# A six-layer feature-cross network rewritten: four groups in flight, batched tails, a row-major last job

## The chip, the cores and the metric

The kernel runs on one core of one Trainium2 chip. The metric is the device time of a run in microseconds (us); a time quoted for a kernel is the median of its runs. The profiled span of a run is some 2 us shorter than its device time, so spans are compared only with spans.

## The reference

```python
B, D, L = 16384, 416, 6        # x0: (B, D), ws: (L, D, D), bs: (L, D), all bf16
x = x0
for l in range(L):
    proj = x @ ws[l] + bs[l]
    x = x0 * proj + x
return x
```

416 is 3 × 128 + 32. The 32 left-over features (the *tail*) shape both kernels: an array of 128 by 128 has to be divided into strips to be used well by them.

## The kernel before

The rows are cut into eight groups of 2048. Inside, the features lie on the partitions, so x is held transposed: three tiles of 128 × 2048, and the tail folded as 128 × 512 (four chunks of 512 rows, 32 features each). One *job* is one layer of one group. TensorE (PE) fills banks of 512 columns in PSUM (the memory that matmuls write to), ScalarE (ACT) *evicts* them, that is, copies them to a buffer in SBUF (the on-chip working memory) with the bias added, and VectorE (DVE) multiplies by x0 and adds x. A *ring* is a set of such buffers used in turn. The core of a job on PE (cut: lines and indentation left out):

```python
for i in range(NMT):                       # three output tiles of 128 features
    rp_first = (i % 2 == 1)
    if rp_first:                           # the 32-row matmuls first, then 12 full ones
        emit_k32(g, l, i, xin3, nb_of, False, first=True)
        emit_full(g, l, i, xin, nb_of, waits_tj, k32_first=True)
    else:
        emit_full(g, l, i, xin, nb_of, waits_tj)
        emit_k32(g, l, i, xin3, nb_of, False)
emit_tail_cp(g, l, xin, jb["tail"])        # the tail: 12 matmuls of 32 columns
emit_tail_bd(g, l, xin3, jb["tail"])       # and one with a block-diagonal weight
```

Four 32-row matmuls run at once in four strips of the array, so a job is 43 *passes* of 512 columns: 3 × (12 + 1) for the tiles, 3 + 1 for the tail. Two groups are in flight at a time. ACT evicts 512 columns at a time into a ring of three wide buffers and, for tails, a ring of two.

```python
NTW = 3      # wide eviction buffers, 128 x 2048
NTS = 2      # tail eviction buffers, 128 x 512
...
for n, bk in enumerate(banks):
    act.wait_ge(sem_pe, n + 1)
    if n == e["first_bank"] and e["ring_wait"]:
        ...
        if e["ring"] == "s" and e["rk"] >= NTS:
            act.wait_ge(sem_dve, small_list[e["rk"] - NTS] + 1)
    ...
    act.activation(dst, src, ACT_F.Identity, bias=bias_ap, scale=1.0).then_inc(sem_act, 1)
```

All x0 come by transposing DMAs from DRAM. The outputs of groups 0 to 5 go through a DRAM scratch and a transposing DMA back; the last two groups are transposed on PE at the end and stored by rows.

## Time and profile before

The time before is 512.78 us (three runs, 512.35 to 512.87). How to read the profile: PE, DVE, ACT and POOL are engines, PEld is the loading of weights for PE, the granted clock is the share of PE's full clock that the chip allowed it at the time ("cold" below means matmuls at a low granted clock), and the "chain" is the chain of work that ended last, followed back from the end. The first fence has lines of the page of the kernel before: its span, busy time by engine, and the chain's shares.

```profile
span 511.6 us, 7778 instructions
...
PE 485.9 (95%) x3069; PEld 198.8 (39%) x3118; DVE 376.9 (74%) x430; ACT 381.9 (75%) x646; POOL 9.5 (2%) x36
...
PE 89%; DVE 3%; issue 2%; DMA 2%; ACT 2%; SPq 1%; DVEq 0%; ACTq 0%
```

PE is busy 95% of the time and carries 89% of the chain. The next fence is the timeline of PE in the kernel before, in mid-run. Its columns: start in us, length in us, engine, line, operation, output and inputs, shape, how many, and in brackets how long the engine stood idle before.

```profile
211.28 0.39 PE L526 MATMUL ps<-x_3_1,w_3 32*128 32x512 bf16 x4
211.60 1.04 PE L504 MATMUL ps<-x_1_0,w_0 128*128 128x512 bf16 x4
...
216.89 0.39 PE L528 MATMUL ps<-x_3_1,w_3 32*128 32x512 bf16 x4
217.21 0.40 PE L539 MATMUL ps<-x_1_0,w_0 128*32 128x512 bf16 x4
...
218.20 1.03 PE L504 MATMUL ps<-x_0_0,w_0 128*128 128x512 bf16 x4 [0.16 <-issue]
```

A job repeats every 9.83 us without a stall. Its 43 passes at 0.216 us are 9.29 us; the rest is five changes of shape (128 rows to 32 rows, to 32 columns, and back) at about 0.105 us each. The Trainium skill ("TensorEngine Tiling (Array Packing)", Key Properties) says that changing the tiling mode drains TensorE; it gives no figure, and this trace agrees and prices it.

The third fence is the view by windows of the kernel before: window, its length, then busy time and number of instructions of PE, PEld, DVE, ACT and POOL, then the granted PE clock, the DMA share and GB/s.

```profile
0.00:27.53 27.53, 19.61 (x91) 7.90 (x93) 3.61 (x4) 8.36 (x14) 2.40 (x16) 1.00 0.86 149
122.34:495.16 372.82, 366.21 (x2285) 147.60 (x2323) 291.79 (x319) 294.72 (x497) 0.00 (x0) 1.00 0.43 107
495.16:511.60 16.44, 7.08 (x128) 6.05 (x127) 10.34 (x34) 7.11 (x16) 0.00 (x0) 0.86 0.65 208
```

In the middle DVE is busy 78% (291.79 of 372.82) and ACT 79%. The second job starts at 27.53, and 16.4 us pass after the last regular matmul (that is, the last matmul of a job, not a transpose of the output).

### The profile page before, as it was taken

To read this page: it belongs to the slowest core of one execution; us is meant where nothing else is said; L and a number is where in the kernel's file an instruction comes from. 1 tells how busy PE (TensorE), PEld (TensorE's weight loads), DVE (VectorE), ACT (ScalarE), POOL (GpSimd) and SP (SyncE) were. 2 spreads that over 40 slices of the span, in tenths; PEclk is the share of its full clock that TensorE was granted. 3 is DMA by queue.
4 is the path that set the end of the run, shared out by engine and by line. 5 is a ranking of instruction groups with operands and counts; after the bars stand their busy time and mean duration, and the time that the engine had idled before them with its cause. 6 is when DMAs were issued, how large, how long until landed. Compare 5 with 4: busy or idle time off the path is not lost.

```text
span 511.6 us, 7778 instructions
## 1 busy us (share of the span) xinstructions
PE 485.9 (95%) x3069; PEld 198.8 (39%) x3118; DVE 376.9 (74%) x430; ACT 381.9 (75%) x646; POOL 9.5 (2%) x36
## 2 busy tenths in 40 slices
PE   5899999999999999999999999999999999999992
PEld 2333343343334334343433433343343343434352
DVE  0167787787788778778787877877887787787795
ACT  1467787787878778787877878787787777878782
POOL 1020200000000000000000000000000000000000
PEclk9999999999999999999999999999999999999998
DMA  9769700000667799000569579000277660000008
GB/s 168 153 150 206 142 2 0 1 1 1 176 168 233 159 209 190 1 0 2 163 156 247 136 200 215 15 2 1 57 218 217 184 168 0 1 1 0 1 2 266
DMA packets 134147, 53.91 MB, mean 105 GB/s; under 512 B 111584, under 2 KB 131808, under 8 KB 134112
## 3 DMA queue, kind: packets, MB, share of 16 engines
q1 hardware_dynamic: 128252, 51.29, 41.9%
q10 hardware_dynamic: 5860, 2.14, 1.8%
q8 instruction: 24, 0.39, 0.3%
q14 instruction: 11, 0.09, 0.0%
HBM read 2.56 MB, written 23.86 MB: 52 GB/s over the span
## 4 chain that ended last, share of the span: by engine, by line
PE 89%; DVE 3%; issue 2%; DMA 2%; ACT 2%; SPq 1%; DVEq 0%; ACTq 0%
PE ps L504 74%; PE ps L539 7%; PE ps L528 6%; PE ps L526 2%; DMA x0T_2<-in_x_dram 2%; ACT tmpw L420 2%; SPq L243 1%; DVE tmpw L743 1%; DVE x_0_1 L704 0%; PE ps L485 0%; DVE x_0_2 L704 0%; DVE x_1_1 L773 0%; DVE x_0_0 L704 0%; PE ps L656 0%; DVE tmpw L738 0%
## 5 line engine op out<-in xcount | busy, mean ns | idle before, releaser
L420 ACT ACTIVATE tmpw<-ps,bias_f 128x512 bf16<-128x512 f32 x576 | 343.7, 698 | 107.4 <-PE ps L528 107.4
L738 DVE TENSOR_TENSOR tmpw<-tmpw,x0T_2 128x2048 bf16<-128x2048 bf16 x47 | 57.6, 1225 | 51.9 <-ACT tmpw L420 51.9
L738 DVE TENSOR_TENSOR tmpw<-tmpw,x0T_1 128x2048 bf16<-128x2048 bf16 x47 | 57.6, 1226 | 48.2 <-ACT tmpw L420 48.2
L738 DVE TENSOR_TENSOR tmpw<-tmpw,x0T_0 128x2048 bf16<-128x2048 bf16 x47 | 57.3, 1219 | 28.6 <-ACT tmpw L420 28.1
L504 PE MATMUL ps<-x_1_0,w_0 128*128 128x512 bf16 x287 | 74.0, 380 | 3.3 <-issue 3.2
L504 PE MATMUL ps<-x_1_1,w_1 128*128 128x512 bf16 x288 | 73.9, 379 | 0.0
L504 PE MATMUL ps<-x_1_2,w_2 128*128 128x512 bf16 x288 | 73.9, 379 | 0.0
L504 PE MATMUL ps<-x_0_0,w_0 128*128 128x512 bf16 x192 | 49.4, 380 | 2.6 <-issue 2.6
L504 PE MATMUL ps<-x_0_1,w_1 128*128 128x512 bf16 x192 | 49.3, 379 | 0.0
L504 PE MATMUL ps<-x_0_2,w_2 128*128 128x512 bf16 x192 | 49.3, 379 | 0.0
L504 PEld LDWEIGHTS ps<-x_1_1,w_1 128*128 128x128 bf16 x288 | 28.2, 98 | 34.0
L504 PEld LDWEIGHTS ps<-x_1_2,w_2 128*128 128x128 bf16 x288 | 28.2, 98 | 34.0
L504 PEld LDWEIGHTS ps<-x_1_0,w_0 128*128 128x128 bf16 x288 | 25.9, 98 | 36.1 <-issue 10.2
L420 ACT ACTIVATE tmps<-ps,bias_f 128x512 bf16<-128x512 f32 x48 | 33.9, 705 | 0.0
L704 DVE TENSOR_TENSOR x_0_0<-tmpw,x_1_0 128x2048 bf16<-128x2048 bf16 (+1 forms) x27 | 29.7, 1099 | 0.0
L704 DVE TENSOR_TENSOR x_0_1<-tmpw,x_1_1 128x2048 bf16<-128x2048 bf16 (+1 forms) x27 | 29.7, 1099 | 0.0
L704 DVE TENSOR_TENSOR x_0_2<-tmpw,x_1_2 128x2048 bf16<-128x2048 bf16 (+1 forms) x27 | 29.7, 1099 | 0.0
L504 PE MATMUL ps<-x0T_0,w_0 128*128 128x512 bf16 x95 | 27.0, 402 | 2.8 <-DMA w_2<-in_ws_dram 1.4
L504 PE MATMUL ps<-x0T_1,w_1 128*128 128x512 bf16 x95 | 26.2, 399 | 3.2 <-DMA x0T_1<-in_x_dram 3.2
L504 PEld LDWEIGHTS ps<-x_0_2,w_2 128*128 128x128 bf16 x192 | 18.8, 98 | 22.7
L504 PEld LDWEIGHTS ps<-x_0_1,w_1 128*128 128x128 bf16 x192 | 18.8, 98 | 22.7
L504 PEld LDWEIGHTS ps<-x_0_0,w_0 128*128 128x128 bf16 x192 | 17.5, 98 | 23.8 <-issue 6.8
(204 smaller groups left out, 393.9 us busy)
## 6 DMA issues: line engine op xcount, KB each, us to landing
out_dram<-ost SPq DMA_DIRECT2D x25, 416.0 KB, 3.4
x6T_scratch<-x_0_0 SPq DMA_DIRECT2D x6, 512.0 KB
x6T_scratch<-x_0_1 SPq DMA_DIRECT2D x6, 512.0 KB
x6T_scratch<-x_0_2 SPq DMA_DIRECT2D x6, 512.0 KB
w_1<-in_ws_dram SPq DMA_DIRECT2D x6, 104.0 KB
w_2<-in_ws_dram SPq DMA_DIRECT2D x6, 104.0 KB
w_0<-in_ws_dram SPq DMA_DIRECT2D x5, 104.0 KB
out_dram<-x_1_0 SPq DMA_DIRECT2D x1, 416.0 KB, 2.7
```

Source lines behind the costliest of these rows:

```text
L243: sp.dma_start_transpose(x0T[s][t][:, :], x0[0:GC, t * P:(t + 1) * P]).then_inc(sem_g0[t], 16)
L420: act.activation(dst, src, ACT_F.Identity, bias=bias_ap, scale=1.0).then_inc(sem_act, 1)
L504: ins = pe.matmul(bank_ap(nb_of[(i, j)]), wm[l][t][:, ecols], xin[t][:, j * CH:(j + 1) * CH], start=(t == 0 and not k32_first), stop=last,)
L526: pe.matmul(bank_ap(nb_of[(i, j)]), lhsT, rhs, start=True, stop=False, tile_position=tp)
L528: pe.matmul(bank_ap(nb_of[(i, j)]), lhsT, rhs, start=False, stop=True, tile_position=tp).then_inc(sem_pe, 1)
L539: ins = pe.matmul(bank_ap(n, j * TAIL, (j + 1) * TAIL), wm[l][t][:, ecols], xin[t][:, j * CH:(j + 1) * CH], start=(t == 0 and not bd_first ...
L704: dve.tensor_tensor(o_ap, t_ap, i_ap, ALU.add).then_inc(sem_dve, 1)
L738: dve.tensor_tensor(tw[:, :], tw[:, :], x0T[s][i][:, :], ALU.mult).then_inc(sem_dm, 1)
L743: dve.tensor_tensor(tw[:, cols], tw[:, cols], x0T[s][i][:, cols], ALU.mult).then_inc(sem_dm, 1)
```

## The change

The intent is to change shape less often, to start and end sooner, and to need no DRAM scratch. The whole kernel is rewritten (a small scheduler derives the waits), so the diff is cut to its core.

1. *Staggered groups.* Jobs run on a diagonal order over up to four groups, so that the tails of four jobs can run in one phase, and 24 full matmuls run between 32-row phases of eight.

```diff
-for r in range(NR):
-    for l in range(L):
-        for q in range(R):
-            units.append(("job", r * R + q, l))
+order = [(0, 0), (0, 1), (1, 0), (0, 2), (1, 1), (2, 0), (0, 3), (1, 2), (2, 1), (3, 0), ...]
+cuts = [1, 2, 3, 4, 4, 4, 4, 4, 4, 4, 4, 4, 3, 2]          # tails per batch
+def tails(batch):
+    bs_ = take(len(batch))                                  # one PSUM bank for each tail
+    for (g, l), b in zip(batch, bs_):
+        ...   # 12 matmuls of 32 columns, 4 with the block-diagonal weight
+        evacuate_tail(g, l, b)                              # ACT, then two DVE instructions
```

2. *Eviction.* ACT mostly takes 1024 columns at a time. Wide buffers go from 3 to 4, tail buffers from 2 to 3. DVE's add of one eviction is held back until after the multiply of the next.

```diff
-    NTW = 3
-    NTS = 2
+    NX0, NXS, NX3, NTW, NTS = 5, 6, 8, 4, 3
+        add("act", ... activation(ts[r][:, :], bank(b), ...), writes=[("ts", r)])       # r: one of NTS
+        add("dve", ... tensor_tensor(ts[r], ts[r], x0 tail, mult), release=True)
+        add("dve", ... tensor_tensor(x3s[so], ts[r], src, add), hold=True)
```

3. *Start.* Group 0 comes by plain loads and is transposed on PE. Layer 1's weights are queued behind group 1, whose tail is copied inside SBUF and waits for a transposing DMA.

```diff
-for t in range(NMT):
-    load_x0_tile_g0(t)                     # transposing DMAs
+for j in range(NJ):
+    add("sp", ... dma_start(x0n[:, j, :, :], perm(g0, j)))   # plain; PE transposes
+load_group(1)                              # 4 transposing DMAs, 4 copies that wait for the last
+load_w(1, "sp")
+load_w(2, "sp")
```

4. *Outputs* of groups 0 to 6: DMA transposes from SBUF to SBUF, then one store of 1.7 MB, all on the sync engine's (SP) queue.

5. *The last job* (group 7, layer 5) is computed with rows on the partitions, so that its result needs no transpose. The bias then varies along the free axis, and comes as one more matmul of a row of ones with a bias row (`brow`). Four passes; each multiplies by the rows of x0 and adds the rows of x.

```diff
+# done_with(g, l), at the end of a group's last layer
+if l == L - 1:
+    output(g)                                              # transposes, then the store
+...
+# after all regular jobs
+for j in range(NJ):
+    add("sp", ... dma_start(x0n7[:, j, :, :], perm(rows7, j)))             # x0 rows of group 7
+    add("sp", ... dma_start(brow[j * T32:j * T32 + 1, :], bs[l:l + 1, :])) # bias row
+for kk in range(KK):
+    if kk % 2 == 0:
+        for j in range(NJ): nat_full(kk, j, bks[j], True)
+        nat_rows(kk, bks, False)                           # needs brow
+        if kk == 0: to_rows(0)                             # PE transposes of x, copied by ACT and DVE
+        for j in range(NJ): nat_out(kk, j, bks[j])         # ACT copy, DVE multiply and add
+    ...
```

## The prediction

> **What bounds the kernel now.** TensorE. The page has PE busy 95% of 511.6 us; the chain of waits is 89% PE. In the timeline at 200 to 230 us a job (one group, one layer) repeats every 9.83 us without a stall: 43 passes of 512 columns at 0.216 us and five changes of tiling shape at about 0.105 us (12 full passes to the 32-row phase: 2.69 us, 2.59 of it passes). The Trainium skill ("TensorEngine Tiling (Array Packing)", Key Properties) says that a mode change drains TensorE; this trace agrees and prices it. ACT and DVE have slack (windows: 79% and 78% busy in the middle). The start costs 17.7 us (second job at 27.53, less 9.83), the end 16.4 us (last regular matmul 495.16, span 511.6).
>
> **Middle.** Counted from the instruction order, shape changes fall from 256 to 169: -9.1 us. The 32x32 tail-copy phases (0.43 us for each of six groups) go: -2.6 us. One of 48 jobs moves into the row-major finish; the 47 others take about 455 us of PE, 9.69 us a job. ACT evicts mostly 1024 columns at a time; DVE keeps about 8 us a job. Neither should bind; I expect PE gap-free.
>
> **Start.** Group 0 comes by plain loads (1.7 MB; plain DMA reached 325 GB/s in the windows at the end) instead of DMA transposes (2.3 to 3.1 us per 512 KB). Data by 9 us, PE transposes and copies to 11, first job to 22.5 with a cold clock. The weights of layer 1 sit on SP behind four DMA transposes and copies that wait for the last: they land near 25, so the second job starts near 25 instead of 27.5. An early tail dependency costs 1.3 us.
>
> **End.** The last regular matmul comes at T = 472. PE cannot leave the first of four row-major passes without the bias row (brow). This row, and x0 of the last group, are issued on SP after the output of group 6, which waits for a DVE add near T+2, four small DMA transposes, then a 1.7 MB store. At 325 GB/s store and loads (3.4 MB) take 10.5 us: the bias row lands near T+18, while PE wants it at T+7: a stall of about 11 us. From there four passes, 48 transposes, ACT/DVE copies and the last store take 17 to 20 us. End about T+35; without the stall T+25, near 497.
>
> **Sum.** 512.8 - 2.5 (start) + 1.3 - 9.1 - 2.6 - 3 (early stalls of the old ramp) + 10 (end, net of the moved job) = 507 us; range 496 to 517. Chances: faster by over 2% 0.30, within 2% 0.63, slower 0.07.
>
> **What would show the steps right or wrong.** Middle: in the timeline, runs of 24 full matmuls between 32-row phases of eight, one 32-column phase per four jobs, 9.69 us a job, no idle before PE. Start: PE waits for w_1 near 22 to 25. End: the waits list a PE wait of about 11 us on the DMA of brow, after the first row-major matmuls, with the 1.7 MB store ahead of it in the queue.
>
> **What would make it wrong.** If the queue serves the bias row earlier, or the SBUF-sourced transposes and the store finish before T, the stall goes: near 497. If SBUF-sourced transposes are much slower than the 3.8 us seen for DRAM-sourced ones, the stall grows. PSUM or eviction waits in the middle (eight banks shared by tiles of four and tail batches) of 0.1 to 0.3 us per tile would add 15 us or more.

## The result, and the profile after

The changed kernel took 532.5 us (531.08 to 533.82) against 512.71 for the kernel before in the same rounds: slower, ratio 1.0384 (95% interval 1.0359 to 1.041). Here and below a ratio is from the runs of the same rounds; it is close to the ratio of the medians, but not quite the same. All outputs are right. These are the lines of the page of the changed kernel that answer to those above.

```profile
span 530.9 us, 7651 instructions
...
PE 486.1 (92%) x3198; PEld 207.0 (39%) x3251; DVE 381.5 (72%) x432; ACT 350.5 (66%) x416; POOL 10.9 (2%) x37
...
PE 65%; DVE 13%; ACT 12%; SPq 5%; DMA 3%; issue 2%; DVEq 0%; ACTq 0%
```

Every engine is still less than fully used, ACT even less than before. But the chain has moved: PE's share falls from 89% to 65%, and DVE and ACT now hold a quarter of it. A cut in three segments of the span shows where the time went:

| segment | before | after |
|---|---|---|
| to the second job's first matmul | 27.5 | 26.1 |
| the next 46 jobs | 457.8 | 460.8 |
| the last job and the output | 26.3 | 44.1 |

(For the kernel before, the 46 jobs end one job period ahead of 495.16, at 485.33; for the changed one, all regular matmuls end at T = 486.83.) So the middle did not get shorter, and the end is 17.8 us longer. The next fence has the lines that matter from the list of waits of the changed kernel: who waited, for whom, total us, how often, the longest.

```profile
ACT tw L359 <- DVE tw L368: 49.1, 38, 1.3
...
ACT ts L384 <- DVE x L388: 25.5, 9, 2.8
...
PE ps L708 <- DMA brow<-in_bs_dram: 12.9, 1, 12.9
...
PE ps L410 <- ACT ts L384: 6.5, 9, 0.7
...
PE ps L398 <- DMA w<-in_ws_dram: 5.5, 1, 5.5
...
PE ps L410 <- DVE x L388: 2.0, 1, 2.0
```

The second of these is regular: nine times 2.8 us, and PE waits for ACT's L384 nine times. (The first, at the wide evictions, is longer in total, but in many short pieces; e1 below shows that it does not hold PE.) L384 is ACT's eviction of a tail, L388 DVE's add that frees a tail buffer. There are nine batches of four tails. One of them, in PE's timeline of the changed kernel:

```profile
214.39 0.83 PE L423 MATMUL ps<-x,wm 128*32 128x512 bf16 x12
...
218.18 2.54 PE L398 MATMUL ps<-x,wm 128*128 128x512 bf16 x11 [0.16 <-issue]
220.65 0.61 PE L410 MATMUL ps<-x,w 32*128 32x512 bf16 x7
221.99 0.39 PE L410 MATMUL ps<-x,w 32*128 32x512 bf16 x1 [0.72 <-ACT ts L384]
222.30 5.35 PE L398 MATMUL ps<-x,wm 128*128 128x512 bf16 x24
...
293.90 0.83 PE L423 MATMUL ps<-x,wm 128*32 128x512 bf16 x12
```

and the timelines of ACT (first two lines) and DVE (third) in the same stretch:

```profile
216.56 1.84 ACT L384 ACTIVATE ts<-ps,bias 128x512 bf16<-128x512 f32 x3
...
221.24 0.69 ACT L384 ACTIVATE ts<-ps,bias 128x512 bf16<-128x512 f32 x1 [2.83 <-DVE x L388]
...
220.79 0.42 DVE L388 TENSOR_TENSOR x<-ts,x 128x512 bf16<-128x512 bf16 x1
```

ACT evicts three tails, one per buffer, and then has to wait for DVE to empty one. It does so at 220.79 + 0.42 = 221.21, and the fourth eviction starts at 221.24. Its bank is the one that PE's eighth 32-row matmul needs, which starts at 221.99, after the fourth eviction (221.24 + 0.69 = 221.93). PE's seven matmuls were done by 221.26, so 0.72 us are idle. Eight jobs (two batches) run from 214.39 to 293.90 with one more window of the same kind inside: 79.51 us, or 9.94 a job. That is worse than the 9.83 of the kernel before, although shapes change less often.

The start, in PE's timeline of the changed kernel:

```profile
26.06 4.80 PE L398 MATMUL ps<-x,wm 128*128 128x512 bf16 x12 [5.48 <-DMA w<-in_ws_dram]
...
49.70 0.40 PE L410 MATMUL ps<-x,w 32*128 32x512 bf16 x4 [2.00 <-DVE x L388]
50.03 7.04 PE L398 MATMUL ps<-x,wm 128*128 128x512 bf16 x24
```

The second job waits 5.48 us for weights. At full clock twelve full matmuls take 2.76 us in the timeline (so at 14.57 in this trace); after this wait they take 4.80, for the clock had dropped (the window view grants 0.56 there). Later a tail wait of 2.00 us is again followed by slow matmuls: 7.04 us for 24, against 5.35 above.

The end: first the queue of SP (the issuing side of the DMAs), then PE's timeline, of the changed kernel.

```profile
488.81 5.00 SPq L508 DMA_TRANSPOSE ost<-x  x4
494.95 0.37 SPq L514 DMA_DIRECT2D out_dram<-ost  x1
495.37 1.85 SPq L646 DMA_DIRECT2D x<-in_x_dram  x1
497.26 1.11 SPq L648 DMA_DIRECT2D brow<-in_bs_dram  x1
...
501.68 0.32 SPq L648 DMA_DIRECT2D brow<-in_bs_dram  x1
```

```profile
486.83 0.37 PE L692 MATMUL ps<-wm,x 128*128 128x416 bf16 x1
...
493.29 0.54 PE L703 MATMUL ps<-w,x 32*128 32x416 bf16 x4
506.72 0.53 PE L708 MATMUL ps<-brow,ones 1*128 1x416 bf16 x4 [12.89 <-DMA brow<-in_bs_dram]
```

The first line is where the row-major finish begins, T. PE wants the bias row at 493.8, T + 7.0, as predicted. SP issues its last part only at 501.68, after four small transposes, the 1.7 MB store and the x0 rows, and PE goes on at 506.72. The Trainium skill ("DMA: Bandwidth & Descriptors", Anatomy of one DMA — SWDGE (gpsimd) path) says that a semaphore wait happens on the issuing sequencer before dispatch, not in the DMA engines. It says so where it describes DMAs issued from GpSimd; these are issued by SP, and this trace agrees for them: none of the loads, which nothing but their place in the program delays (in e5 below another queue issues them at 486.6), is issued before the store, which waits for the transposes. Then the clock, in the window view of the changed kernel:

```profile
506.72:518.00 11.28, 9.17 (x55) 4.81 (x56) 4.59 (x13) 4.68 (x9) 0.00 (x0) 0.50 0.12 39
518.00:530.90 12.90, 7.37 (x74) 4.57 (x72) 7.65 (x23) 5.24 (x11) 0.00 (x0) 0.90 0.31 99
```

For 11.28 us after the wait PE runs at half its clock.

### The profile page after: what moved, and what is told of

Read it like the earlier page. It is cut to its first block, busy times and chain, and to the rows that moved or that the text cites. A ratio compares the mean times of both kernels' runs of the same rounds, so it can differ in the third digit from the quotient of the medians.

```text
span 530.9 us, 7651 instructions
## 1 busy us (share of the span) xinstructions
PE 486.1 (92%) x3198; PEld 207.0 (39%) x3251; DVE 381.5 (72%) x432; ACT 350.5 (66%) x416; POOL 10.9 (2%) x37
## 4 chain that ended last, share of the span: by engine, by line
PE 65%; DVE 13%; ACT 12%; SPq 5%; DMA 3%; issue 2%; DVEq 0%; ACTq 0%
PE ps L398 56%; ACT tw L359 10%; PE ps L410 6%; DVE tw L368 5%; DVE x L373 5%; SPq L295 2%; ACT ts L384 1%; DVE ts L386 1%; PE ps L692 1%; DMA brow<-in_bs_dram 1%; DMA Tb<-in_x_dram 1%; DVE x L388 1%; PE ps L667 1%; DMA w<-in_ws_dram 1%; SPq L646 1%
## 5 line engine op out<-in xcount | busy, mean ns | idle before, releaser
L359 ACT ACTIVATE tw<-ps,bias 128x1024 bf16<-128x1024 f32 (+1 forms) x340 | 307.5, 966 | 117.9 <-PE ps L410 51.1
L398 PE MATMUL ps<-x,wm 128*128 128x512 bf16 x1639 | 375.1, 382 | 11.1 <-DMA w<-in_ws_dram 5.5
L368 DVE TENSOR_TENSOR tw<-tw,x 128x2048 bf16<-128x2048 bf16 (+1 forms) x147 | 173.8, 1182 | 113.5 <-ACT tw L359 110.6
L398 PEld LDWEIGHTS ps<-x,wm 128*128 128x128 bf16 x1692 | 160.1, 98 | 220.5 <-issue 37.8
L373 DVE TENSOR_TENSOR x<-tw,x 128x2048 bf16<-128x2048 bf16 (+1 forms) x147 | 172.7, 1176 | 0.0
L410 PE MATMUL ps<-x,w 32*128 32x512 bf16 x564 | 48.0, 380 | 8.5 <-ACT ts L384 6.5
L384 ACT ACTIVATE ts<-ps,bias 128x512 bf16<-128x512 f32 x47 | 29.7, 695 | 25.5 <-DVE x L388 25.5
L423 PE MATMUL ps<-x,wm 128*32 128x512 bf16 x564 | 38.7, 380 | 0.0
L410 PEld LDWEIGHTS ps<-x,w 32*128 32x128 bf16 x564 | 9.8, 92 | 46.3 <-issue 33.1
L386 DVE TENSOR_TENSOR ts<-ts,x 128x512 bf16<-128x512 bf16 x47 | 19.8, 421 | 0.7
L423 PEld LDWEIGHTS ps<-x,wm 128*32 128x32 bf16 x564 | 13.8, 96 | 15.5 <-issue 3.2
L388 DVE TENSOR_TENSOR x<-ts,x 128x512 bf16<-128x512 bf16 x47 | 19.7, 420 | 0.0
L708 PE MATMUL ps<-brow,ones 1*128 1x416 bf16 x16 | 2.1, 431 | 12.9 <-DMA brow<-in_bs_dram 12.9
```

The lines of the kernel that those rows point to most:

```text
L359: add("act", lambda h, a=a, w=w, b0=b0: h.activation(tw[r][:, a * CH:(a + w) * CH], psum[:, b0 * CH:(b0 + w) * CH], ACT_F.Identity, bias=b ...
L368: add("dve", lambda h, a=a, e=e: h.tensor_tensor(tw[r][:, a * CH:e * CH], tw[r][:, a * CH:e * CH], x0s[s0][:, i * GC + a * CH:i * GC + e * ...
L373: add("dve", lambda h, a=a, e=e: h.tensor_tensor(xs[so][:, i * GC + a * CH:i * GC + e * CH], tw[r][:, a * CH:e * CH], src(i, a, e), ALU.ad ...
L384: add("act", lambda h: h.activation(ts[r][:, :], bank(b), ACT_F.Identity, bias=bias[:, 3, l:l + 1], scale=1.0), reads=[("ps", b), "bias"], ...
L386: add("dve", lambda h: h.tensor_tensor(ts[r][:, :], ts[r][:, :], x0s[s0][:, XW:XW + CH], ALU.mult), reads=[("ts", r)] + x03_toks(s0), writ ...
L388: add("dve", lambda h: h.tensor_tensor(x3s[so][:, :], ts[r][:, :], src, ALU.add), reads=[("ts", r)] + stok, writes=[("x3", so)], hold=True)
```

## The experiments

The theory (A) after reading the trace: three independent costs. The ring of three tail buffers against batches of four stalls PE; the bias row is late because of its place in SP's queue; the second job is late because of its weights' place in that queue. Rivals: DVE or ACT or PSUM is short of capacity in the middle, so that one more buffer only moves the wait; the loads at the end are short of bandwidth, so that their order does not matter; the cold clock, not the wait, is the loss.

In kernels that insert lines the line numbers shift: in e4, e7, e8 and e9 (e3 is shifted in its own way: its L705 is the changed kernel's L703), L406 is the full matmul (L398 above), L418 the 32-row one (L410), and L695, L706 and L711 are the row-major finish.

### e1_ts4: four tail buffers

```diff
-    NX0, NXS, NX3, NTW, NTS = 5, 6, 8, 4, 3
+    NX0, NXS, NX3, NTW, NTS = 5, 6, 8, 4, 4
```

> One buffer more for evicted tails (ts 3 to 4). Theory A (the middle lost its gain to the ring of three ts buffers, which the fourth tail of a batch has to wait for): the nine ACT waits for the DVE add (25.5 us in all, 2.8 each) and the nine PE waits behind them go, the span of eight jobs in the middle falls from 79.5 us to about 77.5, and the time falls by 8 to 9 us, to about 524. Rival B (eight PSUM banks are too few for tiles of four and batches of four tails, whatever the buffers): the PE still waits for an eviction after each batch, eight jobs stay near 79.5 us and the time stays within 2 us of 532.5.

Measured: 521.62 us (521.17 to 523.73), ratio to before 1.0171 (1.015 to 1.0193), 10.9 us less than the changed kernel; 8 to 9 had been expected. Lines of PE's timeline of e1, with the batch and its successor two batches on:

```profile
209.99 0.83 PE L423 MATMUL ps<-x,wm 128*32 128x512 bf16 x12
...
216.25 0.61 PE L410 MATMUL ps<-x,w 32*128 32x512 bf16 x8
...
287.29 0.83 PE L423 MATMUL ps<-x,wm 128*32 128x512 bf16 x12
```

and a line of its list of waits:

```profile
ACT tw L359 <- DVE tw L368: 72.3, 56, 1.3
```

The eight 32-row matmuls run as one group with no idle time before any. Eight jobs take 287.29 − 209.99 = 77.30 us, 9.66 a job; 9.69 had been predicted for a middle without gaps. ACT still waits for DVE, now 72.3 us in all against 49.1 at the wide evictions (the list of waits of both), yet PE does not: neither DVE's throughput nor the number of PSUM banks, which is the same eight, was what held PE. One buffer of 128 × 512 was. The ring explains about 10 of the 10.9 us (nine batches at half of 79.51 − 77.30). In the profiled runs, whose spans differ by 11.7, another 1.7 is luck: after the early tail wait, which e1 has too (2.01 us), its 24 matmuls took 5.35 us, not 7.04.

### e2_ts2: two tail buffers

```diff
-    NX0, NXS, NX3, NTW, NTS = 5, 6, 8, 4, 3
+    NX0, NXS, NX3, NTW, NTS = 5, 6, 8, 4, 2
```

> One buffer less for evicted tails (ts 3 to 2). Theory A: the third and the fourth tail of a batch wait for a DVE add each, the PE loss of 0.9 us per batch becomes about 2.4, the time grows by 12 to 15 us, to about 546. Rival B (PSUM banks): no change beyond 2 us.

Measured: 559.42 us (554.21 to 561.38), ratio 1.0884 (1.0828 to 1.094), 26.9 us more than the changed kernel. The direction is theory A's; the size is about twice its number. PE's timeline of e2, one batch and the matmuls after another, shows why:

```profile
231.29 0.60 PE L410 MATMUL ps<-x,w 32*128 32x512 bf16 x6
232.63 0.39 PE L410 MATMUL ps<-x,w 32*128 32x512 bf16 x1 [0.73 <-ACT ts L384]
234.14 0.38 PE L410 MATMUL ps<-x,w 32*128 32x512 bf16 x1 [1.13 <-ACT ts L384]
...
272.82 7.04 PE L398 MATMUL ps<-x,wm 128*128 128x512 bf16 x24
```

Now the third and the fourth tail both wait, each behind its own turn of DVE, and the batches of three wait as well: 20 waits of ACT and 45.0 us in all, against 9 and 25.5. Where the matmuls after the waits ran at full clock, eight jobs take 82.55 us, 3.04 more than with three buffers: 1.52 a batch, 13.7 for nine, within the 12 to 15 expected. What the expectation left out is the rest. The first batch of three lost 1.9 us besides (tails to tails 32.63 us, 1.7 of it cold, against 29.04), and the second waits as long (1.59 us, the first 1.53): 3.8 for both, an estimate. And after five of the eleven batches the 24 matmuls behind the wait took 7.04 us (four times) or 6.59 instead of 5.35: 8.0 us of cold clock. In sum these are 25.5 of the 25.7 us between the two spans (556.6 and 530.9). The mean granted clock fell accordingly, to 0.954 from 0.966.

### e3_brow: the bias row ahead of the output of group 6

```diff
         if l == L - 1:
+            if g == LAST - 1:
+                for j in range(NJ):
+                    add("sp", ... dma_start(brow[j * T32:j * T32 + 1, :], bs[L - 1:L, :]), lane="brow")
             output(g)
```

(and the same loads removed from the end.)

> Only the four bias rows (3 KB) are issued ahead of the output of group 6; the last group's x0 rows stay behind it. Theory C (PE is held by the bias row, which stands in the SP queue behind a 1.7 MB store and 1.7 MB of loads; x0 is the next to hold): the PE wait of 12.9 us on brow goes and PE passes on without it, but the DVE multiplications wait for x0 until about 506 on the span of the changed kernel; time 517 to 521, about 13 us less. Rival D (the end is slow by its own work, the row-major passes, whatever comes first): under 4 us less.

Measured: 523.93 us (522.86 to 525.57), ratio 1.0211 (1.0187 to 1.0236), 8.6 us less than the changed kernel, where about 13 had been expected. The wait of PE for the bias row is gone, but less was won. Timelines of DVE (first) and PE (second) of e3:

```profile
507.35 0.66 DVE L725 TENSOR_TENSOR x<-x,x 128x416 bf16<-128x416 bf16 x2 [10.00 <-DMA x<-in_x_dram]
...
512.56 1.03 PE L705 MATMUL ps<-w,x 32*128 32x416 bf16 x3 [5.84 <-DVE x L689]
```

The x0 rows stand at the same place in the queue as the bias row did. DVE now waits 10.00 us for them, cannot take its share of the transposes' copies out of PSUM meanwhile, and so PE waits 5.84 us for a bank and is cold again afterwards (4.35 us for 12 matmuls). The wait was moved from one load to its neighbour.

### e4_brow_x0: both loads ahead of that output

```diff
+            if g == LAST - 1:
+                for j in range(NJ):
+                    add("sp", ... dma_start(v7[:, j, :, :], perm(x0[LAST * GC:B, :], j)), lane="n7")
+                    add("sp", ... dma_start(brow[j * T32:j * T32 + 1, :], bs[L - 1:L, :]), lane="brow")
             output(g)
```

> Bias rows and the last group's x0 rows are both issued ahead of the output of group 6. Theory C: no wait for DMA at the end, the PE clock stays up in the last phase, the stretch from the last regular matmul to the end falls from 44.2 us to about 27; time 513 to 516, 17 to 19 us less and 4 us below the run with the bias rows alone. Rival D: under 4 us less.

Measured: 517.81 us (516.49 to 519.56), ratio 1.0091 (1.0067 to 1.0115), 14.7 us less than the changed kernel; 17 to 19 had been expected. In the profiled run, the fastest of the four, the stretch after the last regular matmul takes 27.6 us, about the 27 expected. The window view of e4:

```profile
493.71:506.00 12.29, 10.03 (x112) 6.37 (x108) 7.07 (x20) 6.95 (x12) 0.00 (x0) 0.98 0.66 212
```

Once PE has the bias row at 493.71, the rest takes 514.4 − 493.71 = 20.7 us at a clock of 0.98. In the changed kernel the same work, from 506.72 to 530.9, took 24.2 us, at first at half clock. So the late loads cost 13.0 us of delay (506.72 − 493.71), and the cold clock that they left another 3.5 (24 transposes took 2.75 us instead of 1.53, 12 matmuls 4.28 instead of 2.30): the cold clock is part of the loss, not a rival explanation of it.

### e5_actq: the late loads on ACT's queue, at their old place in the program

```diff
-        add("sp", ...  n7 and brow loads
+        add("act", ... n7 and brow loads
```

> The bias rows and the last group's x0 rows stay at their place in the program, but are issued on ACT's DMA queue instead of SP's. Theory C (what holds PE is the order of one queue, not the DMA engines' capacity): ACT reaches them near 489.5 us, 5 us before the store is issued, and they land by about 495; the PE wait on brow falls from 12.9 us to under 3 and the time to 515 to 519. Rival E (the DMA engines are busy with the output of group 6, so that no queue would bring the rows earlier): the wait stays above 8 us.

Measured: 521.19 us (520.74 to 522.79), ratio 1.0165 (1.0147 to 1.0183), 11.3 us less than the changed kernel and a little short of what was expected (515 to 519). ACT issued them from 486.6 to 489.4, after the large transposes of the output and around the start of the small ones (488.31); SP issued the store only at 495.84. PE's timeline of e5:

```profile
495.13 0.35 PE L708 MATMUL ps<-brow,ones 1*128 1x416 bf16 x4 [1.51 <-DMA brow<-in_bs_dram]
```

The wait falls from 12.89 to 1.51 us though the same bytes move at the end. Bandwidth did not hold the bias row; its place behind the store in SP's order did. The clock was low again after this wait and the next (12 matmuls in 4.35 us, against 2.30 in e4), which is most of what e5 lacks of e4.

### e6_w1: the weights of layer 1 ahead of group 1

```diff
-    load_group(1)
     load_w(1, "sp")
+    load_group(1)
```

> Only the weights of layer 1 are issued on SP before the DMA transposes of group 1 instead of after them. Theory F (the PE waits 5.5 us for these weights, and runs some 2 us cold after it): the second job starts near 21 us instead of 26.1, its first twelve matmuls take 2.6 us instead of 4.8; time 524 to 527, 6 to 8 us less. Rival G (the start is bound by the loads of group 1, whatever their order): the third job waits instead, under 3 us less.

Measured: 526.9 us (525.81 to 527.49), ratio 1.0264 (1.0247 to 1.0281), 5.6 us less than the changed kernel; 6 to 8 had been expected. PE's timeline of e6:

```profile
22.53 1.73 PE L398 MATMUL ps<-x,wm 128*128 128x512 bf16 x6 [1.50 <-DVE x L373]
```

The second job starts near 20 instead of 26.06, but soon waits 1.50 us for DVE to deliver the last x of the first job: the weights had covered a data dependency that lay just behind them.

### e7_all: e1, e4 and e6 together

> Four ts buffers, bias and x0 rows ahead of the output of group 6, weights of layer 1 first, all together. If the three causes are separate, their savings add (10.9 + 14.7 + about 7 us): 498 to 502 us, faster than the kernel before by over 2%, and eight jobs in the middle take 77.3 to 77.8 us. If one hides another, above 504.

Measured: 502.14 us (500.94 to 504.44), ratio to before 0.9794 (0.9765 to 0.9822): about 2% faster than the kernel before, with an interval that straddles the 2% of a verdict, so that the record calls it unclear. The median is just outside the 498 to 502 expected. Against the changed kernel it saves 30.4 us; the three parts alone saved 10.9, 14.7 and 5.6, in sum 31.2. They add up within the spread of the runs, so they are separate costs; eight jobs take 77.30 us here, too. Of the waits that are left, one is known from above, in PE's timeline of e7:

```profile
44.66 0.39 PE L418 MATMUL ps<-x,w 32*128 32x512 bf16 x4 [1.95 <-DVE x L396]
44.98 5.35 PE L406 MATMUL ps<-x,wm 128*128 128x512 bf16 x24
```

It is the early tail wait again. This time the 24 matmuls after it took 5.35 us: a wait of 2 us left the clock low in some profiled runs (changed kernel, e2, e3, e4, e6: 7.04 us) and not in others (e1, e5, e7: 5.35).

### e8_all_t2 and e8b_repeat: e7, and the tails of a two-job batch one tile earlier

The scheduler moves a tail phase past one tile so that tiles come in pairs. For the batch of two in the ramp (the first jobs, before four groups are in flight) this puts the tails close before the 32-row matmuls that need their result. The edit also moves the tails of the last batch, the other one of two jobs.

```diff
-            if single % 2 == 0:
+            if single % 2 == 0 and len(items[k][1]) != 2:
```

> As the run with all three, and the tails of the two batches of two jobs run a tile earlier. Theory: the PE wait of 2.0 us for a tail's DVE add near 48 us goes, with 1.7 us of cold matmuls behind it, and the DVE backlog before the row-major finish shrinks by 1 to 2 us: 494 to 497 us. Rival: these waits only move to the next DVE result, under 1.5 us less than the run with all three.

> The best version so far again, as the yardstick for the next run on the same chip: 496 to 499 us.

Measured: 497.32 us (496.96 to 498.37), ratio 0.9698 (0.9683 to 0.9712), faster; the same kernel again in five rounds 497.01 us (496.78 to 500.43), ratio 0.9708 (0.9682 to 0.9733). That is 4.8 us less than e7, and e8 itself is just above the 494 to 497 expected. The wait of 1.95 us is gone; the regular matmuls end 2.9 us earlier than in e7 (470.14) and the finish after them is 1.4 us shorter. In span terms e8 reaches the second job at about 19.95 instead of 27.53, ends its regular matmuls at 467.28 (46 jobs in 447.3 us, against 457.8 before), and then needs 27.7 us to 495.0, where the kernel before needed 26.3. The row-major finish, with its loads on time, was still no gain. PE's timeline of e8b shows one reason:

```profile
477.73 1.59 PE L706 MATMUL ps<-w,x 32*128 32x416 bf16 x4 [2.12 <-ACT x L724]
```

The first matmuls of the second pass wait for banks that ACT has not emptied, because ACT's copies of the first pass were queued behind its copies of the transposes. The next 12 full matmuls took 3.86 us, though after the same wait in e4 they took 2.30.

### e9_copy_first: e8, and ACT's copies of the first pass ahead of those of the transposes

```diff
             if kk == 0:
+                for j in range(NJ):
+                    nat_copy(kk, j, bks[j])        # ACT: PSUM to SBUF
                 to_rows(0)
             for j in range(NJ):
-                nat_out(kk, j, bks[j])
+                nat_out(kk, j, bks[j], kk == 0)    # multiply and add only, where copied
```

> As the yardstick, but in the row-major finish ACT copies the first pass's four results out of PSUM before it copies the transposed rows. Theory: PE's second pass waits 2.1 us for these banks (and runs its twelve matmuls cold after it, 4.0 us for 2.3); with the copies first the wait goes, 2 to 4 us less, 493 to 495. Rival: the finish is paced by DVE and ACT in sum, so the order changes nothing beyond 1 us.

Measured: 493.85 us (492.65 to 496.1), ratio to before 0.9625 (0.961 to 0.9641), 3.2 us less than e8b in the same rounds. PE's timeline of e9:

```profile
478.44 0.70 PE L706 MATMUL ps<-w,x 32*128 32x416 bf16 x4
...
479.26 2.30 PE L695 MATMUL ps<-wm,x 128*128 128x416 bf16 x12
```

The wait is gone and the 12 matmuls take 2.30 us. The finish is now 493.9 − 470.98 = 22.9 us, shorter than the 26.3 of the kernel before. (In the profiled run, at 496.1 us the slowest of the five, the first job started about 3 us later than in e8b, waiting for its weights, so ends are to be compared from the last regular matmul on.) This is the best version: 3.75% faster than the kernel before.

The kernels of all rounds side by side (the kernel before had medians of 512.59 to 513.31 in them, so the last column is good to about 1 us):

| kernel | us | against the changed kernel |
|---|---|---|
| before | 512.71 | −19.8 |
| changed | 532.5 | |
| e1, four tail buffers | 521.62 | −10.9 |
| e4, late loads early | 517.81 | −14.7 |
| e6, weights early | 526.9 | −5.6 |
| e7, the three | 502.14 | −30.4 |
| e8, and tails earlier | 497.32 | −35.2 |
| e9, and copies first | 493.85 | −38.6 |

## Why the prediction was wrong, point by point

The prediction was 507 us, range 496 to 517; the changed kernel took 532.5.

**What it had right.** PE bounded the kernel before, and the arithmetic of passes and shape changes holds: e1, e7 and e8 run the middle at 9.66 us a job, where 9.69 was predicted. The stall of PE for the bias row was named with its cause (12.9 us measured, about 11 predicted), and PE reached it at T + 7.0 as said. The wait for the second job's weights was named, too (26.06 against 25).

**The step that failed: "Neither should bind; I expect PE gap-free."** It was argued from busy shares, and ACT's did fall, from 75% to 66%. What bound was a ring: three tail buffers against batches of four. The fourth eviction waited 2.83 us for DVE to free a buffer, held the PSUM bank all that while, and each such batch cost PE 1.11 us of its 39.8 (79.51 − 77.30, for two), in nine batches about 10 us. e1 took the ring's limit away and won 10.9; e2 tightened it and lost 26.9, some 8 of it cold clock. The prediction's last paragraph did name PSUM and eviction waits as a risk, but its sum gave them nothing. Had the schedule of one batch been written out (three evictions, then a fourth that needs a DVE add held back behind other work), the diff alone would have shown that the fourth must wait.

**Terms of the sum that were mis-sized.**
- The regular matmuls were to end at T = 472; they ended at 486.83, 14.8 us later. The ring is about 10. The second job started 1.1 later than predicted. Cold matmuls after the weights' wait cost 2.0 (4.80 − 2.76), a term that was missing. The early tail dependency was put at 1.3 and cost 3.7: 2.0 of wait, 1.7 of cold clock (7.04 − 5.35). Counting what lies above the prediction's own terms (10, 1.1, 2.0 and 2.4), these make 15.5; about 0.7 us was won elsewhere.
- The end was to take 35 us after T and took 44.1. The bias row came at T + 19.9, not T + 18, and the rest took 24.2 us instead of 17 to 20. Of it, 3.5 us were the cold clock, which the prediction left out though it had just predicted the long wait that brings it about.
- "Without the stall T + 25" was also too good: with the loads on time e8 needed 27.7, until the order of ACT's copies was mended (22.9 in e9).
- The last 1.6 us: the sum was compared with device time, while T and the rest are of the span (530.9 against 532.5). 14.8 + 9.1 + 1.6 = 25.5, the whole miss.

**The expected gain, then,** was there in full in the middle and was eaten by waits that the rewrite brought: e9 has the rewrite's structure with five small mends.

**What stays open.** Why the same wait of 2 us left the clock low in the changed kernel, e2, e3, e4 and e6 and not in e1, e5 and e7, and likewise why only five of e2's eleven batches were followed by cold matmuls. Each kernel has one trace, so how often this happens from run to run is not known either.

## What to carry to other kernels

When work is batched, check that every ring that a batch passes through holds the whole batch, or that its buffers come free before the last piece needs one: three buffers for four tails cost 2% of this kernel, on engines that were 66% and 72% busy, so count buffers along the schedule of one batch instead of reading busy shares. A queue is an order, not only a bandwidth: a small load that nothing delays (a bias row, a weight) belongs ahead of any transfer that waits for computed data, together with its neighbours, or the wait only moves to them. Price a PE wait as itself plus the cold clock that may follow (here 2 to 3.5 us for waits of 5 to 13 us, and up to 1.7 after some waits of 2 us or less), and when one wait is taken away look for the dependency just behind it.

## What the Trainium skill lacked or had wrong

- "TensorEngine Tiling (Array Packing)", Key Properties, says that a mode change drains TensorE but not what it costs: about 0.105 us a change in the kernel before (five a job: 9.83 − 43 × 0.216 = 0.54 us).
- "TensorE: Matmul & The Clock Gate" advises, in its table of why this matters, no PE gaps above about 3 us. A gap of about 2 us was enough here in five traces (24 matmuls in 7.04 us) and not in three (5.35 us); in e2 gaps of 0.73 and 1.13 us, with one matmul between them, were enough in four of nine batches. (The page's own case of PSUM-queue cycling says that frequent short idle can do this; the advice in the table leaves it out.) Its Part 1 calls the window of about 3.4 us free-running and the ramp run-variable; that fits, but no run here isolates it.
- The same page puts the warm-up at about 3.4 us of sustained work. After the bias row's wait the window view grants 0.50 for 11.28 us, in which PE was busy 9.17 us, 2.75 us of it with transposes and much of the rest with short runs and gaps. Part 4's remark that transposes do not count as PE-busy fits; it was not tested apart. Where it says that full clock does not engage for them, the traces differ: in the changed kernel 24 transposes took 2.75 us at 507.19, at half clock, and 1.50 us at 518.38, after the clock had risen.
- "DMA: Bandwidth & Descriptors", Latency and other measured facts, gives an effective bandwidth for DMA transposes (261 GB/s in one kernel), which says nothing of small ones; its other figures for them are sequencer cycles, in its part on trn3. Here, from SBUF to SBUF, three of 512 KB took 7.89 us on the issuing queue (1.57 MB, so 199 GB/s), but four of 32 KB took 5.00 us, 1.25 us each or 26 GB/s. These are times of issue; the landing comes later.
- No page read says that an eviction ring shorter than a batch stalls PE through the PSUM bank it holds: 1.11 us a batch here, about 10 us in all. The nearest, "Perfetto Trace Analysis", Identifying Performance Opportunities, says only that a gap which keeps repeating can mean too little SBUF or PSUM (buffer count, tile sizes).
